# Attention into soft experts on one core: q transposed by PE, scores in 64x32 tiles, phi's sums by two-column products

## The chip, the cores and the metric

The kernel runs on one core of a Trainium2 chip. A time is the device time of one execution in microseconds (us). PE is the matrix engine, DVE, ACT and POOL are the vector, scalar and general engines; SP issues the loads and stores. All data are 32-bit floats.

## The reference

Inputs are q, k, v of shape (8 batches, 8 heads, 576 positions, 64) and phi (8, 8, 576, 32). Phi's softmax pools keys and values to 32 memory slots per head; q attends to those; the result, taken as 4608 rows of 512, goes through a soft mixture of 8 experts with 4 slots each.

```python
a = np.exp(phi - np.max(phi, axis=2, keepdims=True))      # max over the positions
a = a / (np.sum(a, axis=2, keepdims=True) + 1e-09)
k_m = np.einsum('bhsm,bhsd->bhmd', a, k)
v_m = np.einsum('bhsm,bhsd->bhmd', a, v)
scores = scale * np.matmul(q, k_m.transpose(0, 1, 3, 2))
attn = np.exp(scores - np.max(scores, axis=-1, keepdims=True))
attn = attn / (np.sum(attn, axis=-1, keepdims=True) + 1e-09)
x = np.matmul(attn, v_m)                                  # then (b*s, h*d)
logits = x @ phi_moe
d = softmax(logits, over rows); slot_input = d.T @ x
slot_out[e] = np.maximum(slot_input[e] @ w1[e], 0.0) @ w2[e]
return softmax(logits, over slots) @ slot_out
```

## The kernel before, in words

The 8 batches go in four pairs. A batch's q, k, v and phi lie with 128 partitions = two heads x 64 row groups, four quarters c of two heads each, and 9 consecutive positions j per row group (P = 128, HALF = 64, Y = M = 32, J = 9, C = 4).

For each batch, `pool_phi` takes the maximum of phi over positions (DVE L511, PE transposes and broadcasts it at L519 and L533, ACT copies it at L544), subtracts it on POOL (L549) and exponentiates on ACT (L555). The sum over positions is a tree of four additions on POOL (L562) and one product with a mask on PE (L572); DVE forms the reciprocal (L579, L580). `pool_kv` multiplies phi's exponentials with k and v on PE, 72 products in 64x32 tiles, into the two banks of `kvbank` (L599); ACT scales the sums out by the reciprocal (keys L615, values L622). PE transposes the keys (L635, four blocks) and values (L640), ACT copies them (L654, L645), and `vpp` prepares values against the expert router's weights (L662, copied at L675).

q is transposed by DVE in 32x32 blocks (L700), two instructions per batch. That puts the two halves of the 64 head dimensions beside each other, so a score is the sum of two products with 32-deep key blocks; the keys are padded with zeros to hold one 32-row block apart from the other (`kps`, cleared once at L419), and each set of scores (one quarter c of a pair) is 8 products in 64x64 tiles into `scbank` (L716). DVE transposes the set (L730), and `softmax` runs over DVE (L746, L761, L770, L777), POOL (L751, L774) and ACT (L756, L766). `logits` multiplies by the prepared values (L785). After each pair, `route` forms the pair's share of the expert input (L803 to L922, among it the products at L849, L875 and L909). When the last pair is in, SIM, the experts' input, is finished on DVE (L1000); the experts follow on PE (L1064, L1113) with weights of 1 MB each, and the output is formed (L1220) and stored.

What sets the order: every step is handed to a `Plan` with an engine, an assumed cost and its inputs and outputs. The planner plays the program through with those costs, takes for each engine the ready step of the lowest phase, and writes the instructions out in that order; the order on every engine is fixed before the run. Buffers come from pools (`Slots`); a step waits for a free one. `b_m` has three PSUM banks, `b_l` one for the logits, `b_s2` one pair of banks (`scbank`) for the scores, `b_kv` is `kvbank`. On idle PE the plan puts fill products of ones (L476) in the first 25 us and near the end of the attention. SP issues the loads in plan order; k, v, phi and q have two buffers each, the weights lie over buffers that earlier stages have left.

## Time and profile before

| what | us |
|---|---|
| median of three runs (lowest, highest) | 224.25 (222.32, 224.52) |
| the profiled execution's own time | 221.83 |
| its span, first to last instruction | 220.1 |
| busy: PE / DVE / POOL / ACT | 172.5 / 135.5 / 86.7 / 71.4 |
| granted PE clock, mean | 0.916 |
| read from HBM, written | 66.65 MB, 9.44 MB |

In a row of the timeline stand the start, the length, engine, line, operation, output from input, tile sizes and count, and in brackets how long the engine stood idle before it and what it waited for. A group's row has busy us and mean ns of one instruction. A plain fp32 product is two matmul instructions; a transpose by PE is one. Line numbers of before and of the changed kernel differ by 1 to 25.

### The profile page before, as it was taken

How to read it: one execution, taken by the hardware profiler on the slowest of the kernel's cores; microseconds unless marked ns; L12 is line 12 of the kernel's file. 1: busy time of each engine (PE TensorE's matmuls, PEld its weight loads, DVE VectorE, ACT ScalarE, POOL GpSimd, SP SyncE). 2: the span in 40 equal slices, each digit the busy share in tenths (PEclk: the TensorE clock that was granted, in tenths of full speed). 3: DMA queues.
4: the chain of work that ended last, by engine and by line, in shares of the span. 5: the costliest groups of instructions: out<-in, count | busy, mean ns of one | idle time of the engine just before them, and what ended most of it. 6: DMA issues, size and time to landing. Idle time of an engine off the chain costs nothing.

```text
span 220.1 us, 5624 instructions
## 1 busy us (share of the span) xinstructions
PE 172.5 (78%) x2418; PEld 105.3 (48%) x2418; DVE 135.5 (62%) x230; ACT 71.4 (32%) x182; POOL 86.7 (39%) x85
## 2 busy tenths in 40 slices
PE   8997977695798988598988799629999975599400
PEld 6676745354564654356654387415554340065100
DVE  6825048969459999879658965499102860268500
ACT  2041234542516626337342340201002331168400
POOL 6298019596934992999623641030000000000000
PEclk9999999979699999999969999976999999769755
DMA  6999999999999999999596493999999998049997
GB/s 215 383 395 390 380 392 381 390 380 390 385 388 389 388 406 380 389 392 406 194 410 212 188 420 102 401 350 327 395 413 410 408 409 320 3 179 411 415 415 295
DMA packets 27881, 76.45 MB, mean 347 GB/s; under 512 B 1744, under 2 KB 5840, under 8 KB 27856
## 3 DMA queue, kind: packets, MB, share of 16 engines
q1 hardware_dynamic: 27856, 76.09, 91.1%
q8 instruction: 19, 0.31, 0.6%
q14 instruction: 6, 0.05, 0.1%
HBM read 66.65 MB, written 9.44 MB: 346 GB/s over the span
## 4 chain that ended last, share of the span: by engine, by line
PE 41%; DMA 22%; DVE 14%; POOL 9%; issue 5%; ACT 2%; SPq 1%; DVEq 0%; POOLq 0%
DMA top<-in_q_dram 10%; DMA arena<-in_moe_w_dram 9%; PE bank L1064 7%; PE kvbank L476 6%; PE bank L785 5%; PE scbank L716 4%; PE bank L1220 4%; PE kvbank L599 3%; DMA out_dram<-arena 3%; DVE arena L700 3%; POOL arena L774 3%; POOL arena L562 3%; PE bank L849 2%; PE kvbank L1113 2%; POOL arena L751 2%
## 5 line engine op out<-in xcount | busy, mean ns | idle before, releaser
L549 POOL TENSOR_TENSOR arena<-arena 128x1152 f32<-128x1152 f32 x8 | 21.0, 2632 | 16.0 <-ACT arena L544 13.3
L476 PE MATMUL kvbank<-ones 128*128 128x256 f32 x92 | 25.4, 419 | 2.2 <-ACT arena L622 1.1
L700 DVE STREAM_TRANSPOSE arena<-top 128x1152 f32<-128x1152 f32 x16 | 21.7, 1361 | 7.1 <-DMA top<-in_q_dram 7.1
L774 POOL TENSOR_TENSOR arena<-arena,ssm 128x576 f32<-128x576 f32 x16 | 18.5, 1162 | 15.6 <-DVE ssm L770 15.5
L562 POOL TENSOR_TENSOR arena<-arena 128x128 f32<-128x128 f32 (+2 forms) x32 | 23.4, 731 | 2.3 <-ACT arena L555 0.3
L716 PE MATMUL scbank<-arena 64*64 64x288 f32 x256 | 21.6, 433 | 3.0 <-DVE arena L730 2.5
L785 PE MATMUL bank<-arena 128*128 128x288 f32 x64 | 21.4, 464 | 2.6 <-DVE arena L777 2.6
L751 POOL TENSOR_TENSOR arena<-arena,smx 128x576 f32<-128x576 f32 x16 | 18.4, 1158 | 11.5 <-DVE smx L746 11.5
L599 PE MATMUL kvbank<-arena 64*32 64x128 f32 x1152 | 20.2, 273 | 2.2 <-issue 1.5
L476 PEld LDWEIGHTS kvbank<-ones 128*128 128x128 f32 x92 | 18.1, 207 | 6.7 <-issue 1.6
L511 DVE TENSOR_REDUCE arena<-arena 128x128 f32<-128x1152 f32 x8 | 17.0, 2138 | 5.6 <-DMA arena<-in_phi_dram 5.6
L599 PEld LDWEIGHTS kvbank<-arena 64*32 64x32 f32 x1152 | 16.2, 106 | 6.3 <-issue 3.9
L1064 PE MATMUL bank<-arena,SIM 128*32 128x256 f32 x256 | 16.4, 421 | 3.4 <-DVE SIM L1000 3.4
L1113 PE MATMUL kvbank<-arena 128*32 128x512 f32 x128 | 15.6, 598 | 2.9 <-DMA arena<-in_moe_w_dram 2.9
L730 DVE STREAM_TRANSPOSE arena<-scbank 128x576 f32<-128x576 f32 x16 | 12.2, 765 | 8.9 <-PE scbank L716 8.9
L785 PEld LDWEIGHTS bank<-arena 128*128 128x128 f32 x64 | 12.1, 206 | 8.1 <-DVE arena L777 3.8
L1220 PE MATMUL bank<-sr,cT 128*128 128x512 f32 x36 | 13.2, 505 | 3.1 <-DVE sr L1207 1.4
L1231 DVE COPY arena<-bank 128x512 f32<-128x512 f32 x18 | 11.8, 691 | 4.7 <-DMA out_dram<-arena 2.4
L777 DVE STREAM_TRANSPOSE arena<-arena 128x576 f32<-128x576 f32 x16 | 12.1, 758 | 3.8 <-POOL arena L774 3.7
L716 PEld LDWEIGHTS scbank<-arena 64*64 64x64 f32 x256 | 9.0, 137 | 10.8 <-DVE arena L730 4.5
L756 ACT ACTIVATE arena<-arena 128x576 f32<-128x576 f32 x16 | 11.0, 688 | 8.4 <-POOL arena L751 8.4
L1064 PEld LDWEIGHTS bank<-arena,SIM 128*32 128x32 f32 x256 | 8.6, 121 | 10.7 <-DVE SIM L1000 3.6
(104 smaller groups left out, 234.4 us busy)
## 6 DMA issues: line engine op xcount, KB each, us to landing
arena<-in_moe_w_dram SPq DMA_DIRECT2D x32, 1024.0 KB, 9.9
top<-in_q_dram SPq DMA_DIRECT2D x8, 1152.0 KB, 13.8
arena<-in_k_dram SPq DMA_DIRECT2D x8, 1152.0 KB, 11.2
arena<-in_v_dram SPq DMA_DIRECT2D x8, 1152.0 KB, 13.6
out_dram<-arena SPq DMA_DIRECT2D x12, 768.0 KB, 7.6
arena<-in_phi_dram SPq DMA_DIRECT2D x8, 576.0 KB, 8.7
arena<-in_moe_phi_dram SPq DMA_DIRECT2D x1, 64.0 KB, 4.8
```

What stands on the lines that cost most here:

```text
L476: lambda: nc.tensor.matmul(warm.ap, ones, ones.unsqueeze(1).to_broadcast([P, 2, P]), start=True, stop=True,),
L549: lambda: nc.gpsimd.tensor_tensor(ph(), ph(), mb.ap.unsqueeze(2).to_broadcast([P, C, J, M]), op=ALU.subtract),
L562: plus = lambda o, x, y: nc.gpsimd.tensor_tensor(o, x, y, op=ALU.add)
L599: nc.tensor.matmul(acc.ap[M * c: M * c + M, a, : 2 * D], ph()[h0: h0 + HALF, c, j, :], kv()[h0: h0 + HALF, :, c, j * D: j * D + D], start= ...
L700: nc.vector.transpose(qT.ap.rearrange("p (i u y) -> p u i y", i=2, y=Y), qt.ap[:, h * QT_SZ: h * QT_SZ + QT_SZ].rearrange("p (u i x) -> p ...
L716: nc.tensor.matmul(scb.ap[HALF * g: HALF * g + HALF, a, :JY], kb[g].ap[h0: h0 + HALF, i, c].rearrange("p r m -> p (r m)"), qT[g][c // 2].a ...
L751: lambda: nc.gpsimd.tensor_tensor(exv(), exv(), bc(mx), op=ALU.subtract),
L774: lambda: nc.gpsimd.tensor_tensor(exv(), exv(), bc(sm), op=ALU.mult),
L785: nc.tensor.matmul(lp.ap[:, :JY], vpb.ap[:, h, :], aT.ap[:, a * JY: (a + 1) * JY], start=(h == 0), stop=(h == H - 1),)
L1064: nc.tensor.matmul(hb.ap[NS * j: NS * j + NS, :256], SIM.ap[:, 2 * i + c, NS * e: NS * e + NS], wv[:, c, 256 * j: 256 * j + 256], start=(e ...
L1113: nc.tensor.matmul(pacc.ap[NS * x: NS * x + NS, 0, :DM], hT()[:, 4 * t + 2 * i + j, NS * e: NS * e + NS], wv[:, j, t, :], start=(e == 0 an ...
L1220: lambda po=po, i=i, ct=cT[bp, j0]: nc.tensor.matmul(po.ap[:, :DM], ct.ap()[:, i * P: i * P + P], sr.ap, start=True, stop=True),
```

## The change

Four things change together.

q: each batch's q is transposed by PE in 128x128 blocks, two positions of one head pair at a time (L707); the ninth position of two quarters is done by two plain products with the identity (L699). Three blocks go into one of two new PSUM slots, `b_q`, the last 384 columns of each bank of `kvbank`, and ACT copies them out (L712). There are six such groups per batch.

Scores: with all 64 dimensions in partitions a score is one product with the plain keys, in 64x32 tiles: 16 products of 160 or 128 columns per set (L733). Even and odd positions lie apart, DVE turns the set in two pieces (L746), and `POS` undoes the order of positions at the end. The zero padding of the keys goes; PE transposes two key blocks instead of four (L624).

Phi's sums: POOL's tree goes; PE multiplies each of the 9 positions and 4 quarters of phi's exponentials with the two-column mask, 36 products in 128x32 tiles (L564).

Fill products go to the free columns of `scbank`, 192 columns instead of 256.

```diff
-    b_kv = Slots([kvbank])
+    b_kv = Slots([kvbank], [(10, 1)])
+    b_q = Slots([kvbank[:, i, P:] for i in range(2)], [(10, 1), (10, 1)])
+    b_acc = Slots([kvbank], [(10, 1)], (b_kv, b_q))
...
-    NWARM = 40
+    NWARM = 52
...
-            plus(t, ph()[:, :, 0:4, :], ph()[:, :, 4:8, :])
-            plus(t[:, :, 0:2], t[:, :, 0:2], t[:, :, 2:4])
-            plus(t[:, :, 0], t[:, :, 0], t[:, :, 1])
-            plus(es.ap, t[:, :, 0], ph()[:, :, 8, :])
...
+            for j in range(J):
+                for c in range(C):
+                    nc.tensor.matmul(
+                        sp.ap[M * c: M * c + M, :2], ph()[:, c, j, :], maskhp,
+                        start=(j == 0), stop=(j == J - 1), tile_position=(0, M * c),
+                    )
...
-                nc.vector.transpose(
-                    qT.ap.rearrange("p (i u y) -> p u i y", i=2, y=Y),
-                    qt.ap[:, h * QT_SZ: h * QT_SZ + QT_SZ].rearrange("p (u i x) -> p u i x", i=2, x=Y),
-                )
...
+                    for i in range(3):
+                        o = tp.ap[:, i * P: i * P + P]
+                        k = 3 * x + i
+                        if k == JH:
+                            for c in range(2):
+                                nc.tensor.matmul(
+                                    o[HALF * c: HALF * c + HALF],
+                                    qv[:, 2 * h + c, (J - 1) * D: J * D],
+                                    ident, start=True, stop=True,
+                                    tile_position=(0, HALF * c),
+                                )
+                        else:
+                            c, j = (0, k) if k < JH else (1, k - JH - 1)
+                            nc.tensor.transpose(
+                                o, qv[:, 2 * h + c, 2 * j * D: 2 * (j + 1) * D], ident
+                            )
...
+                    nc.scalar.copy(qT.ap[:, 3 * P * x: 3 * P * (x + 1)], tp.ap)
...
+                    for r in range(R):
+                        for s in range(2):
+                            n, b, _ = blocks(s)
+                            h0, x = HALF * s, HALF * g + Y * r
+                            nc.tensor.matmul(
+                                scb.ap[x: x + Y, s, n * Y * a: n * Y * a + n * Y],
+                                kb[g].ap[h0: h0 + HALF, a, c, :],
...
+            turn(0)
+            turn(1)
...
-                add(DVE, dve(QT_SZ), f, r=[qt], w=[t])
+                        add(PE, 0.36, f, r=[qt.part(h), ident_b], w=[tp], also=[t])
+                        add(ACT, act(3 * P), copy, r=[tp], w=[part])
```

What the planner makes of it is seen at two places on PE and one on ACT. On PE right after the scores of pair 0's last quarter, before:

```order
L716 MATMUL scbank<-arena 64x288 x8
L662 MATMUL bank_62<-mphd,arena 64x64 x4
L785 MATMUL bank_65<-arena 128x288 x4
L599 MATMUL kvbank<-arena 32x128 x72
L519 MATMUL bank_63<-ident,arena 128x128
L572 MATMUL bank_64<-maskhp,arena 128x2
L533 MATMUL bank_62<-ident,pmh_82 64x128 x2
L785 MATMUL bank_65<-arena 128x288 x2
```

Changed, from the same place:

```order
L707 MATMUL kvbank<-ident,top 128x128 x4
L699 MATMUL kvbank<-ident,top 64x128 x2
L707 MATMUL kvbank<-ident,top 128x128
L624 MATMUL bank_63<-ident,arena 128x128 x2
L631 MATMUL bank_62<-ident,arena 128x128
L520 MATMUL bank_64<-ident,arena 128x128
L707 MATMUL kvbank<-ident,top 128x128 x6
L807 MATMUL bank_65<-arena 128x288 x2
```

Pair 1's q blocks now stand between the keys' transposes, phi's maximum and pair 0's logits, where before the next pooling followed.

On PE ahead of pair 3's first scores (`top` is q, `kvbank` the pooled sums and the q blocks), before:

```order
L785 MATMUL bank_65<-arena 128x288 x2
L599 MATMUL kvbank<-arena 32x128 x24
L875 MATMUL bank_62<-rep,arena 128x32 x4
L881 MATMUL bank_62<-rep,arena 128x32 x2
L572 MATMUL bank_64<-maskhp,arena 128x2
L909 MATMUL bank_63<-arena 64x128 x4
L785 MATMUL bank_65<-arena 128x288 x2
L635 MATMUL bank_62<-ident,arena 128x4x32 x4
L640 MATMUL bank_64<-ident,arena 128x128
L716 MATMUL scbank<-arena 64x288 x8
```

Changed:

```order
L564 MATMUL bank_64<-maskhp,arena 32x2 x36
L592 MATMUL kvbank<-arena 32x128 x72
L807 MATMUL bank_65<-arena 128x288 x2
L707 MATMUL kvbank<-ident,top 128x128
L699 MATMUL kvbank<-ident,top 64x128 x2
L707 MATMUL kvbank<-ident,top 128x128 x4
L624 MATMUL bank_63<-ident,arena 128x128 x2
L631 MATMUL bank_62<-ident,arena 128x128
L807 MATMUL bank_65<-arena 128x288 x2
L707 MATMUL kvbank<-ident,top 128x128 x3
L653 MATMUL bank_64<-mphd,arena 64x64 x4
L733 MATMUL scbank<-arena 32x160
```

Phi's sums stand ahead of the pooling instead of behind it, and q groups between the last pooling and the scores.

On ACT ahead of the same scores (`prs` is phi's reciprocal), before:

```order
L615 ACTIVATE arena<-kvbank,prs_85 128x4x32 x2
L622 ACTIVATE arena<-kvbank,prs_85 128x64 x2
L922 COPY arena<-bank_63 128x128
L766 ACTIVATE ssm_81<-ssm_81 128x18
L654 COPY arena<-bank_62 128x512
L645 COPY arena<-bank_64 128x256
L675 COPY arena<-bank_63 32x8x32 x2
```

Changed:

```order
L712 COPY arena<-kvbank 128x384 x2
L788 ACTIVATE ssm_81<-ssm_81 128x18
L608 ACTIVATE arena<-kvbank,prs_85 128x128 x2
L613 ACTIVATE arena<-kvbank,prs_85 128x64 x2
L712 COPY arena<-kvbank 128x384 x2
L636 COPY arena<-bank_62 128x256
L645 COPY arena<-bank_63 128x256
L712 COPY arena<-kvbank 128x384
L666 COPY arena<-bank_64 32x8x32 x2
```

The q copies (L712) stand in front of, between and behind the steps that take the pooled sums out, and behind exponentials of the scores (L778).

On SP the loads keep their order but for one weight load, which moves from behind batch 5's q to ahead of batch 5's phi, k and v, and one that now stands between the q loads of batches 6 and 7.

More of the change, by code (lines that the diff above doesn't have):

```diff
@@ L324 @@
     PHI_SZ, KV_SZ = C * J * M, 2 * C * J * D
-    Q_SZ, QT_SZ = C * J * D, C * J * D // 2
-    KP_W = R * (P + Y)
+    Q_SZ, QT_SZ = C * J * D, J * P
+    JH = J // 2
+    QB = J * P
+    POS = [j // 2 if j % 2 == 0 else (J + 1) // 2 + j // 2 for j in range(J)]
     EX_SZ = PC + JN
@@ L466, in first @@
         return FIRST.index(name) - 90000 if name in FIRST else None
-    warm = Tile(ap=kvbank[:, 1, 256:512])
+    warm = Tile(ap=scbank[:, 1, 320:512])
     def fill(n, pri, r=()):
@@ L652, in pool_kv @@
         add(
-            ACT, act(4 * P),
-            lambda: nc.scalar.copy(kd.ap.rearrange("p i c r m -> p (i c r m)"), tp.ap),
+            ACT, act(2 * P),
+            lambda: nc.scalar.copy(kd.ap.rearrange("p a c m -> p (a c m)"), tp.ap[:, : 2 * P]),
             r=[tp], w=[kd],
@@ L685, in load_q @@
     def load_q(b):
-        qt = qs.tile()
+        qt = qs.tile().split(2)
         load(
@@ L696, in q_blocks, with f, copy @@
         for h in range(2):
-            qT = qTs.tile()
-            def f(h=h, qT=qT):
-                nc.vector.transpose(
-                    qT.ap.rearrange("p (i u y) -> p u i y", i=2, y=Y),
-                    qt.ap[:, h * QT_SZ: h * QT_SZ + QT_SZ].rearrange("p (u i x) -> p u i x", i=2, x=Y),
-                )
-            halves.append((qT, f))
+            qT = qTs.tile().split(3)
+            for x in range(3):
+                tp = b_q.tile()
+                def f(h=h, x=x, tp=tp):
+                    qv = qt.ap.rearrange("p (c j d) -> p c (j d)", c=C, j=J)
+                    for i in range(3):
[11 more added lines that the diff above has]
+                            c, j = (0, k) if k < JH else (1, k - JH - 1)
+                            nc.tensor.transpose(
+                                o, qv[:, 2 * h + c, 2 * j * D: 2 * (j + 1) * D], ident
+                            )
+                def copy(x=x, tp=tp, qT=qT):
+                    nc.scalar.copy(qT.ap[:, 3 * P * x: 3 * P * (x + 1)], tp.ap)
+                halves.append((h, qT, qT.part(x), tp, f, copy))
         return halves
@@ L727, in scores, with blocks @@
-        add(PE, 1.0, f, r=[qT[0][c // 2], qT[1][c // 2], *kb], w=[scb], also=[ex])
-        add(
-            DVE, dve(PART),
-            lambda: nc.vector.transpose(
-                ex.ap[:, c * PART: (c + 1) * PART].rearrange("p (a x) -> p a x", a=2),
-                scb.ap[:, :, :JY],
-            ),
-            r=[scb], w=[ex.part(c)],
-        )
+        def blocks(s):
+            n = JH + (s == c % 2)
+            b = 0 if c % 2 == 0 else JH + 1 - s
+            pos = 0 if s == 0 else J - n
+            return n, b, pos
@@ new lines, in f @@
+        def f():
+            for a in range(2):
+                for g in range(2):
+                    for r in range(R):
[5 more added lines that the diff above has]
+                                kb[g].ap[h0: h0 + HALF, a, c, :],
+                                qT[g][c // 2].ap.rearrange("p (b x) -> p b x", b=J)[
+                                    h0: h0 + HALF, b: b + n,
+                                    HALF * a + Y * r: HALF * a + Y * r + Y,
+                                ],
+                                start=True, stop=True, tile_position=(h0, x),
+                            )
@@ new lines, in scores, with turn, f @@
+        add(PE, 0.6, f, r=[qT[0][c // 2], qT[1][c // 2], *kb], w=[scb], also=[ex])
+        def turn(s):
+            n, _, pos = blocks(s)
+            nc.vector.transpose(
+                ex.ap[:, c * PART: (c + 1) * PART].rearrange("p (a x) -> p a x", a=2)[
+                    :, :, pos * Y: (pos + n) * Y
+                ],
+                scb.ap[:, s, : 2 * n * Y].rearrange("p (a x) -> p a x", a=2),
+            )
+        def f():
+            turn(0)
+            turn(1)
+        add(DVE, 2 * dve(PART // 2), f, r=[scb], w=[ex.part(c)])
@@ L939 @@
             qt = load_q(2 * bp + g)
-            hs.append([(qt, *x) for x in q_blocks(qt)])
+            hs.append((qt, q_blocks(qt)))
         for h in range(2):
@@ L943 @@
             for g in range(2):
-                qt, t, f = hs[g][h]
-                add(DVE, dve(QT_SZ), f, r=[qt], w=[t])
-        qT = [[x[1] for x in y] for y in hs]
+                qt, blocks = hs[g]
+                for half, t, part, tp, f, copy in blocks:
+                    if half == h:
+                        add(PE, 0.36, f, r=[qt.part(h), ident_b], w=[tp], also=[t])
+                        add(ACT, act(3 * P), copy, r=[tp], w=[part])
+        qT = [[y[0][1], y[3][1]] for _, y in hs]
         ex = sexs.tile().split(C)
@@ L1051, in load_w @@
         return t
-    pacc = b_kv.tile()
+    pacc = b_acc.tile()
     def expert_in(e, hb):
```

56 lines of the change are left out of this document (13 added, 43 removed).

## The prediction

> **What bounds the kernel now.** I read the chain of waits from its end first, since it says which stretch fixes the time.
>
> ```profile
> 20.63 0.63 ACT arena L615 x2
> 21.26 0.42 ACT arena L622 x2
> ...
> 147.32 0.30 DVE SIM L1000
> 147.67 10.18 PE bank L1064 x144
> ...
> 158.21 6.18 PE bank L1064 x112
> ...
> 168.59 18.81 DMA arena<-in_moe_w_dram
> ...
> 200.37 7.29 DMA out_dram<-arena
> ```
>
> From SIM on, at 147.6 us, the end is a row of expert products, expert weights still arriving, and output. The change touches none of that, so I let those 72.5 us (220.1 less 147.6) stand and ask when SIM is ready. The next view is the busy time by stretches; two are cut at the first scores (L716) of pair 0 and of pair 3. Its columns after the stretch are its length, then busy us of PE, weight loads, DVE, ACT and POOL, granted clock, DMA share, GB/s.
>
> ```profile
> 50.00:60.00 10.00, 5.90 (x140) 4.29 (x130) 7.44 (x12) 3.30 (x10) 8.11 (x8) 0.83 1.06 389
> ...
> 80.00:90.00 10.00, 7.72 (x106) 4.35 (x104) 8.56 (x15) 4.37 (x13) 5.59 (x4) 1.00 1.03 385
> 31.30:114.60 83.30, 68.43 (x1333) 44.23 (x1331) 67.20 (x103) 36.60 (x101) 60.16 (x54) 0.94 1.01 378
> 114.60:135.60 21.00, 19.23 (x169) 12.55 (x169) 15.00 (x26) 6.52 (x20) 9.16 (x8) 1.00 0.67 257
> ```
>
> In the 83.3 us from 31.3, the first scores of pair 0, to 114.6, those of pair 3, three pairs of batches go round. No engine is full: PE 68.4, DVE 67.2, POOL 60.2. PE's 68.4 at a mean clock of 0.94 are 64.3 us of full-clock work; the other 19.0 are 14.9 of standing still and 4.1 of cold clock. What it stands still for, and one wait of ACT's and one of the loads', are in the list of waits (total us, times, longest):
>
> ```profile
> ACT arena L615 <- PE kvbank L476: 4.2, 1, 4.2
> ...
> PE bank L519 <- DVE arena L511: 5.9, 5, 2.4
> ...
> PE bank L785 <- DVE arena L777: 2.6, 4, 1.8
> ...
> PE scbank L716 <- DVE arena L730: 2.5, 5, 0.9
> SPq L458 <- PE kvbank L599: 46.0, 7, 10.4
> ```
>
> PE waits for DVE above all, so taking work off DVE and POOL can help; but the k and v loads wait for PE's pooling (L599), so PE's own queue paces the supply. The bound is the weave of three engines, and the change moves work to one that has 15 us left.
>
> **The change part by part.** The prices of PE come from starts in its timeline, one row's start to the next row's:
>
> ```profile
> 15.78 2.24 PE L599 MATMUL kvbank<-arena 64*32 64x128 f32 x144
> 17.95 1.13 PE L476 MATMUL kvbank<-ones 128*128 128x256 f32 x4
> ...
> 28.69 0.84 PE L599 MATMUL kvbank<-arena 64*32 64x128 f32 x34 [0.66 <-issue]
> ...
> 31.31 1.46 PE L716 MATMUL scbank<-arena 64*64 64x288 f32 x16
> ...
> 60.80 0.68 PE L662 MATMUL bank<-mphd,arena 128*64 128x64 f32 x8
> 61.41 1.24 PE L785 MATMUL bank<-arena 128*128 128x288 f32 x4
> ...
> 64.41 1.20 PE L716 MATMUL scbank<-arena 64*64 64x288 f32 x16
> 65.54 0.28 PE L810 MATMUL bank<-ident,arena 128*32 128x128 f32 x1
> ...
> 68.06 0.66 PE L635 MATMUL bank<-ident,arena 128*128 128x128 f32 x4
> 68.56 0.27 PE L640 MATMUL bank<-ident,arena 128*128 128x128 f32 x1
> ...
> 78.58 0.66 PE L909 MATMUL bank<-arena 128*64 128x128 f32 x8
> 79.17 1.24 PE L785 MATMUL bank<-arena 128*128 128x288 f32 x4
> 80.25 0.28 PE L572 MATMUL bank<-maskhp,arena 128*128 128x2 f32 x2
> 80.45 0.85 PE L599 MATMUL kvbank<-arena 64*32 64x128 f32 x38
> ...
> 100.30 0.60 PE L635 MATMUL bank<-ident,arena 128*128 128x128 f32 x4
> 100.73 0.27 PE L640 MATMUL bank<-ident,arena 128*128 128x128 f32 x1
> ...
> 114.61 1.73 PE L716 MATMUL scbank<-arena 64*64 64x288 f32 x16
> ...
> 139.17 1.65 PE L849 MATMUL bank<-arena 64*32 64x288 f32 x36 [1.16 <-DVE m L969]
> ```
>
> *q by PE.* Half a batch is 8 transposes of 128x128 and two plain 64-column products (four instructions, since a plain fp32 product is two). L635 makes four such transposes in 0.50 us (68.06 to 68.56), 0.43 at best (100.30 to 100.73); L909 eight such instructions in 0.59. So 8 x 0.125 + 4 x 0.074 = 1.3 us, and a pair has four halves: +5.2 us.
>
> *Scores.* A set takes 1.13 us now (64.41 to 65.54). The new one is 32 instructions of 144 columns on average, on eight tiles. L599 does 144 on eight such tiles with 128 columns in 2.17 us, 15.1 ns each, so 17 ns here: 0.54 us. L849, the same tiles with 288 columns read in runs of 32 as the new ones are, takes 1.65 for 36; halved for the columns 23 ns: 0.73. I take 0.62, between. Four sets: -2.0 us.
>
> *Keys.* Two transposes less per batch: 4 x 0.125 = -0.5 us per pair.
>
> *Phi's sums.* One product of 0.20 us (80.25 to 80.45) goes; 36 products, 72 instructions of two columns on four tiles, come. Bounds: L599's 15.1 ns gives 1.09 us per batch, and L1064, four tiles with 256 columns, 6.18/112 = 55 ns, gives 3.97. I take 18 ns, 1.3 us, near the lower end: the weight loads are as wide as L599's, and the 128 columns that fill its time shrink to two. Two batches: +2.2 us. [...]
>
> Together 5.2 - 2.0 - 0.5 + 2.2 = +4.9 us of PE per pair, 14.7 for three: 64.3 + 14.7 = 79.0 of the old 83.3. (Lowest +3.6: transposes 0.43 for four, scores 0.54, sums 1.09. Highest +10.6: scores 0.73, sums 3.97.)
>
> ```profile
> L562 POOL TENSOR_TENSOR arena<-arena 128x128 f32<-128x128 f32 (+2 forms) x32 | 23.4, 731 | 2.3 <-ACT arena L555 0.3
> L700 DVE STREAM_TRANSPOSE arena<-top 128x1152 f32<-128x1152 f32 x16 | 21.7, 1361 | 7.1 <-DMA top<-in_q_dram 7.1
> ...
> L730 DVE STREAM_TRANSPOSE arena<-scbank 128x576 f32<-128x576 f32 x16 | 12.2, 765 | 8.9 <-PE scbank L716 8.9
> ...
> L1175 ACT CAST cT<-bank 128x384 fp32r<-128x384 f32 x12 | 5.1, 484 | 8.1 <-PE bank L1170 8.1
> ...
> L955 DVE STREAM_TRANSPOSE L<-bank 128x288 f32<-128x288 f32 x4 | 1.9, 480 | 4.9 <-PE bank L785 4.9
> ```
>
> *The other engines.* DVE loses L700, 21.7/4 = 5.4 us per pair, and turns the scores in two pieces of about 0.48 (L955) instead of one of 0.765: +0.2 a set, 0.8 a pair. 67.2 - 3 x 4.6 = 53. POOL loses L562, 5.9 a pair: about 43. ACT gains 12 copies of 128x384 a pair, 0.484 each (L1175): +5.8, about 54. So in this stretch all three have at least 29 us to spare and PE becomes the longest queue. What ends PE's waits is then ACT and the banks: the new q blocks lie in the two banks of kvbank behind the pooled sums. That work on other columns there holds a reader up is in the list above (L615 waited 4.2 us for fills, L476, that wrote other columns); so a q block behind a pooling waits for the pooled sums to be scaled out, 0.63 + 0.42 = 1.05 us (L615, L622), and a pooling for the last q copies. I count one such wait uncovered per pair, 1.0, plus 0.4 for turning scores (two pieces, no second score bank) and 0.4 for a q copy queued on ACT behind an exponential that POOL has not fed: 1.8, 5.4 for three. Cold clock in the old ratio, 4.1/14.9 of that: 1.5. The stretch becomes 79.0 + 5.4 + 1.5 = 85.9 us, 2.6 longer.
>
> *Start and end.* Ahead of 31.3 nothing changes: the last piece of pair 0's pooling (28.69) waited for nothing that PE does, it is v still arriving; the new q blocks and sums fit where fills run now. Cover gone, batch 1's sums alone would cost 1.3. One weight load now stands ahead of batch 5's phi, k and v: 1 MB at 385 GB/s (the row 80 to 90), 2.7 us. I put it at nothing, since two buffers let a load run ahead of its pooling; without that cover it costs its 2.7 us. From 114.6 to SIM: four sets save 2.0, their turning costs 0.8, pair 3's second q halves take about 0.4 of the path: -0.8. Key padding and its DVE memsets go at nothing, in the wait for the first phi.
>
> ```profile
> span 220.1 us, 5624 instructions
> ```
>
> So SIM is 2.6 - 0.8 = 1.8 us later: span 221.9. The profiled execution took 221.83 for its 220.1, and the median of the runs, 224.25, stands 2.4 above it: 223.6 by the profile, 226.0 by the median.
>
> **The rivals.** About 1%, 2.2 us, is what a measurement here can tell from no change.
>
> *Forecast: PE takes the bound over and gives back what DVE and POOL save.* 226, its own range 222 to 230. Chance 0.48, of it 0.25 within 1%, 0.19 above, 0.04 below.
>
> *PE runs almost without a stop.* For it: PE's waits above are nearly all for DVE, which gets 14 us back, and q blocks can go wherever PE would stand. Against: every queue is in a fixed order, and the banks are shared. With the low costs, 64.3 + 10.8 = 75.1, 2 us of standing, 0.5 cold: 77.6, 5.7 shorter, and -0.8 at the end: 217.8. Chance 0.28.
>
> *The two-column products do not overlap (slower).* Their place is L564, ahead of each pooling, so they stand before the k and v loads as well. L662's instructions, all on one tile, take 76 ns (60.80 to 61.41, eight); if only two of the four tiles run at once, 38 ns, 2.74 us per batch, 1.44 more for each of six batches: 8.6, 234.6. It decides from about 20 ns on. Against: L1064's 55 ns for 256 columns needs all four at once. Chance 0.15.
>
> *The clock falls.* PE at 59% busy was granted 0.83 (50 to 60), at 77% 1.00 (80 to 90). [...] Half of 79.0 us at 0.83 costs 79.0 x 0.5 x 0.205 = 8.1, less the 1.5 counted: 232.6. Chance 0.09. [...]
>
> **The numbers.** Predicted 226. Faster: 0.04 + 0.28 = 0.32; within 1%: 0.25 and 0.01 of the last two, 0.26; slower: 0.42. The range 217 to 235 leaves out the ends of the first and third rivals' costs.
>
> **What would show it.** In the new profile L564 should take about 1.3 us per batch, L733 0.62 a set, three L707 0.38; first scores of pair 3 near 117 us, SIM near 149; PE 90% or more busy between, DVE, ACT and POOL under 65%; 72 to 73 us from SIM to the end. First scores of pair 3 before 112 make the second case true; L564 over 1.6 us the third; a clock under 0.9 with PE busy the fourth. The forecast is wrong in kind if SIM moves and the end doesn't, or if PE waits more than 10 us for ACT.

## The result, and the profile after

The changed kernel takes 266.82 us, the kernel before 224.03 beside it: a ratio of 1.189, with a 95% interval of 1.177 to 1.200. I had predicted 226.0, with a range of 217 to 235. The profiled execution took 266.59 us for a span of 264.8. Here and below a time is the median of all runs, while a ratio leaves out the runs that fell in a second, slower state.

The same cuts as before, at the first scores of pair 0 and of pair 3 and at SIM, in the view by stretches of the changed kernel (length, busy us of PE, weight loads, DVE, ACT, POOL, granted clock, DMA share, GB/s):

```profile
0.00:41.50 41.50, 32.15 (x560) 25.11 (x561) 9.51 (x17) 13.30 (x31) 9.53 (x14) 0.84 0.85 303
41.50:156.10 114.60, 90.42 (x2077) 64.45 (x2075) 56.68 (x106) 49.01 (x134) 43.18 (x30) 0.84 0.74 266
156.10:192.60 36.50, 25.39 (x299) 16.07 (x296) 21.54 (x44) 9.15 (x30) 11.19 (x9) 0.86 0.68 253
192.60:264.80 72.20, 50.11 (x462) 23.14 (x462) 29.70 (x63) 18.44 (x37) 0.00 (x0) 0.88 0.84 336
```

The first row grew from 31.3 to 41.5 us, the stretch of three pairs from 83.3 to 114.6, the third from 33.0 to 36.5; the fourth is 72.2 where it was 72.5. All 45 us were lost ahead of SIM. In the stretch PE is busy 90 of 114.6 us, at a clock of 0.84 where it was 0.94. The list of waits of the changed kernel for PE in that stretch (total, times, longest) names what it stands still for:

```profile
PE kvbank L592 <- issue: 16.2, 8, 3.2
PE kvbank L707 <- ACT arena L712: 2.4, 3, 0.9
PE kvbank L707 <- ACT arena L613: 1.9, 2, 1.2
PE scbank L733 <- DVE arena L746: 1.9, 3, 1.0
```

L592 is the pooling (L599 before). "Issue" means that nothing shown was awaited. The page of the changed kernel has the whole run, group by group, and the traffic of the queues:

```profile
q8 instruction: 26, 0.43, 0.7%
...
L592 PE MATMUL kvbank<-arena 64*32 64x128 f32 x1152 | 26.2, 322 | 21.6 <-issue 19.9
```

The line for q8 counts packets that carry instructions, 26 of them; the kernel before has this line:

```profile
q8 instruction: 19, 0.31, 0.6%
```

PE's timeline of the changed kernel at the first stop and at two later ones shows where it stands (start, us, what; in brackets the idle time ahead):

```profile
15.27 0.55 PE L707 MATMUL kvbank<-ident,top 128*128 128x128 f32 x3 [0.62 <-ACT arena L712]
15.65 1.47 PE L477 MATMUL scbank<-ones 128*128 128x192 f32 x8
17.05 0.78 PE L564 MATMUL bank<-maskhp,arena 128*32 128x2 f32 x72
17.75 1.34 PE L592 MATMUL kvbank<-arena 64*32 64x128 f32 x76
22.74 2.35 PE L592 MATMUL kvbank<-arena 64*32 64x128 f32 x68 [3.64 <-issue]
...
45.03 0.77 PE L733 MATMUL scbank<-arena 64*32 64x160 f32 x32 [1.00 <-DVE arena L746]
45.80 0.78 PE L564 MATMUL bank<-maskhp,arena 128*32 128x2 f32 x72
49.69 3.38 PE L592 MATMUL kvbank<-arena 64*32 64x128 f32 x128 [3.11 <-issue]
54.52 0.45 PE L592 MATMUL kvbank<-arena 64*32 64x128 f32 x16 [1.45 <-issue]
```

The stops are in the middle of one row of products, once after 76, once before the first, once after 128. The trace shows nothing that is awaited there. Counting all PE records of the trace (each fp32 product is two MATMUL and two LDWEIGHTS: the eight poolings of 72 products are 1152 of each), and setting beside them the packets of the instruction queue, 16,384 bytes each, gives:

```
PE's record   multiple of 256   PE stands (us)        packet in flight   PE after landing
at the stop   behind 449
   449            0             19.09 to 22.74  3.64   20.22 to 21.33      1.40 us
   705            1             26.03 to 26.59  0.56   24.11 to 25.20      1.38
  1473            4             46.58 to 49.69  3.11   47.22 to 48.31      1.38
  1729            5             53.07 to 54.51  1.45   52.11 to 53.19      1.32
  2241            7             71.84 to 74.56  2.72   72.18 to 73.29      1.27
  2753            9             88.05 to 88.71  0.66   86.19 to 87.29      1.42
  3009           10             90.74 to 92.44  1.70   89.75 to 90.97      1.47
  3777           13            108.28 to 110.26 1.98  107.73 to 108.80     1.46
  4289           15            126.34 to 129.52 3.18  127.01 to 128.12     1.40
  5057           18            148.65 to 150.06 1.40  147.60 to 148.69     1.37
```

Every stop lies at a multiple of 256 records, and every time PE goes on 1.3 to 1.5 us after a packet has landed. Together 20.4 us, of which 19.8, all but the stop at 26.03, lie on the chain of work that ended last. I read them as PE having run out of instructions.

The kernel before stops so twice, 0.66 us at record 705 and 0.83 at 2497, again 256 times 1 and 8 behind 449. The first is the row at 28.69 that the prediction quotes; its packet was in flight from 26.09 to 27.18, and PE went on 1.5 us later. The second is this row:

```profile
82.14 0.43 PE L599 MATMUL kvbank<-arena 64*32 64x128 f32 x10 [0.83 <-issue]
```

The rest of this document calls that *standing*: idle time of PE at such a multiple (within 3 records, since a few are missing) that ends 1.1 to 1.7 us after an instruction packet lands.

### The profile page after: what moved, and what is told of

Read it like the earlier page. It is cut to its first block, busy times and chain, and to the rows that moved or that the text cites. A ratio compares the mean times of both kernels' runs of the same rounds, so it can differ in the third digit from the quotient of the medians.

```text
span 264.8 us, 7589 instructions
## 1 busy us (share of the span) xinstructions
PE 198.1 (75%) x3388; PEld 128.8 (49%) x3388; DVE 117.4 (44%) x228; ACT 89.9 (34%) x230; POOL 63.9 (24%) x53
## 4 chain that ended last, share of the span: by engine, by line
PE 59%; DMA 11%; issue 9%; DVE 8%; ACT 6%; POOL 1%; DVEq 0%; ACTq 0%
PE kvbank L592 10%; PE kvbank L707 9%; DMA arena<-in_moe_w_dram 7%; PE bank L807 6%; PE bank L1089 6%; PE scbank L733 4%; PE scbank L477 4%; PE bank L871 3%; ACT arena L712 3%; PE bank L1245 3%; DMA out_dram<-arena 3%; PE kvbank L699 3%; PE bank L653 2%; PE kvbank L1138 2%; PE bank L564 2%
## 5 line engine op out<-in xcount | busy, mean ns | idle before, releaser
L592 PE MATMUL kvbank<-arena 64*32 64x128 f32 x1152 | 26.2, 322 | 21.6 <-issue 19.9
L707 PE MATMUL kvbank<-ident,top 128*128 128x128 f32 x128 | 28.8, 337 | 6.8 <-ACT arena L712 4.7
L592 PEld LDWEIGHTS kvbank<-arena 64*32 64x32 f32 x1152 | 21.0, 124 | 25.0 <-issue 22.2
L712 ACT COPY arena<-kvbank 128x384 f32<-128x384 f32 x48 | 21.6, 483 | 28.5 <-PE kvbank L707 27.4
L707 PEld LDWEIGHTS kvbank<-ident,top 128*128 128x128 f32 x128 | 17.2, 164 | 18.2 <-ACT arena L712 8.8
L796 POOL TENSOR_TENSOR arena<-arena,ssm 128x576 f32<-128x576 f32 x16 | 18.4, 1158 | 27.9 <-DVE ssm L792 27.9
L746 DVE STREAM_TRANSPOSE arena<-scbank 128x320 f32<-128x320 f32 (+1 forms) x32 | 13.5, 460 | 18.6 <-PE scbank L733 14.5
L477 PE MATMUL scbank<-ones 128*128 128x192 f32 x70 | 18.0, 402 | 1.9 <-DVE ones L420 1.1
L608 ACT ACTIVATE arena<-kvbank,prs 128x128 f32<-128x128 f32 x16 | 5.0, 364 | 37.0 <-PE kvbank L592 25.6
L807 PEld LDWEIGHTS bank<-arena 128*128 128x128 f32 x64 | 12.7, 218 | 7.1 <-DVE arena L799 3.4
L477 PEld LDWEIGHTS scbank<-ones 128*128 128x128 f32 x70 | 14.3, 236 | 3.5 <-DVE ones L420 1.1
L733 PE MATMUL scbank<-arena 64*32 64x128 f32 (+1 forms) x512 | 13.1, 301 | 1.9 <-DVE arena L746 1.9
```

The source lines that it names most:

```text
L477: lambda: nc.tensor.matmul(warm.ap, ones, ones[:, :96].unsqueeze(1).to_broadcast([P, 2, 96]), start=True, stop=True,),
L592: nc.tensor.matmul(acc.ap[M * c: M * c + M, a, : 2 * D], ph()[h0: h0 + HALF, c, j, :], kv()[h0: h0 + HALF, :, c, j * D: j * D + D], start= ...
L707: nc.tensor.transpose(o, qv[:, 2 * h + c, 2 * j * D: 2 * (j + 1) * D], ident)
L712: nc.scalar.copy(qT.ap[:, 3 * P * x: 3 * P * (x + 1)], tp.ap)
L733: nc.tensor.matmul(scb.ap[x: x + Y, s, n * Y * a: n * Y * a + n * Y], kb[g].ap[h0: h0 + HALF, a, c, :], qT[g][c // 2].ap.rearrange("p (b x ...
L796: lambda: nc.gpsimd.tensor_tensor(exv(), exv(), bc(sm), op=ALU.mult),
```

## The experiments

Two theories stood first. A: the 144 records a batch of phi's sums, run through in 0.70 us, and the pooling's 288 right behind them use up the packets faster than they come. B: q's blocks lie in the pooling's banks, and the loads of k, v and q, which wait for PE, come late for that. Line numbers differ a little from kernel to kernel: the pooling is L590, L592, L593, L596, L601 or L602 in the rows below.

One thing limits what the runs can tell. When the planner is given other steps or costs, it writes another order for every engine; so it is in tree, before72, sums18, before18, tcopy2, tnoqplan, tnoq0 and tplan. In wide, quarter, shift, tnoq, tnocopy and split the order is the one of the kernel that was edited, but for what is added or left out.

| run | what it is | us | ratio to before, 95% |
|---|---|---|---|
| tree | changed, phi's sums by POOL again | 249.62 | 1.116 [1.108, 1.125] |
| before72 | before, with phi's 72-record sums alone | 246.29 | 1.098 [1.091, 1.106] |
| sums18 | changed, sums by 128-column products | 254.42 | 1.135 [1.129, 1.141] |
| before18 | before, sums by 128-column products | 229.92 | 1.028 [1.019, 1.037] |
| shift | changed, 124 records more ahead | 265.27 | 1.175 [1.168, 1.183] |
| wide | changed, sums 128 columns wide | 260.28 | 1.153 [1.145, 1.162] |
| quarter | changed, a quarter of the loads | 251.98 | 1.113 [1.102, 1.124] |
| tcopy2 | tree, half the q copies on DVE | 249.72 | 1.106 [1.097, 1.115] |
| tnoq | tree, no q blocks from pair 1 on | 236.75 | 1.060 [1.049, 1.072] |
| tnocopy | tree, no q copies from pair 1 on | 240.36 | 1.071 [1.062, 1.080] |
| tnoqplan | tnoq, order written anew | 233.60 | 1.044 [1.032, 1.055] |
| tnoq0 | tnoqplan, pair 0's q by DVE | 237.48 | 1.058 [1.048, 1.067] |
| tplan | tree, order written anew | 256.55 | 1.142 [1.131, 1.152] |
| split | before, scores' products cut in two | 227.34 | 1.014 [1.003, 1.024] |
| qdve | before, new scores and keys alone | 228.18 | 1.021 [1.015, 1.028] |

### One part at a time

*tree* undoes the sums:

```diff
-        for j in range(J):
-            for c in range(C):
-                nc.tensor.matmul(sp.ap[M * c: M * c + M, :2], ph()[:, c, j, :], maskhp, ...)
+        plus(t, ph()[:, :, 0:4, :], ph()[:, :, 4:8, :])
...
+        nc.tensor.matmul(sp.ap[:, :2], es.ap.rearrange("p c m -> p (c m)"), maskhp, ...)
```

> The changed kernel with one part undone: phi's sums go back to the tree of four additions on POOL and one product on PE, so that 144 PE instructions (72 products and their weight loads) leave each batch; q's transposes, the copies and the new scores stay. Theory A (instruction supply: PE's instructions come in packets of 256, and PE stands wherever it runs through a packet in less than about 5 us): PE has 5666 instructions in place of 6818, the idle 'issue' time ahead of the pooling products falls from 19.9 us to under 4, and the time falls to 226 to 242 us. Rival B (q's copies and the pooling share the two banks of kvbank, and the loads of k, v and q come late for that): the sums are only 0.7 us a batch of PE, and the time stays at 255 us or more.

*before72* is the same edit the other way round, in the kernel before.

> The kernel before with this part of the change alone: phi's sums by 72 two-column products a batch on PE, POOL's tree gone; q is still transposed by DVE and the scores are the old ones. Theory A: PE has 1152 instructions more, now stands still inside the pooling at every second or third packet, and the time rises to 236 to 252 us, with 8 to 20 us of 'issue' ahead of the pooling products. Rival B: nothing of q's has been touched, so kvbank is free as before; the sums cost 0.7 us a batch at most and the time is 222 to 231 us.

tree took 249.62, between the two expectations; before72 took 246.29, where only A had it. The list of waits of before72 has one great row for PE, and its timeline shows the same picture with q untouched:

```profile
PE kvbank L590 <- issue: 25.3, 7, 5.0
```

```profile
42.46 0.78 PE L562 MATMUL bank<-maskhp,arena 128*32 128x2 f32 x72
43.17 1.37 PE L590 MATMUL kvbank<-arena 64*32 64x128 f32 x80
49.57 1.75 PE L590 MATMUL kvbank<-arena 64*32 64x128 f32 x56 [5.03 <-issue]
```

So the sums alone, 0.71 us of PE a batch, cost 21.5 us: 25.6 of standing against 1.5 before, more than the 8 to 20 that A expected. A is right for them. But tree is 24.8 us over the kernel before with the sums gone, and PE stands for only 7.3 of its span by the count above. More than half of the loss has a second cause, taken up further below.

### More work in fewer or longer instructions

*sums18* has the sums made by 9 products whose weights are the two columns of the mask and whose 128 columns are phi's; the result is turned back by one transposition.

```diff
-            for c in range(C):
-                nc.tensor.matmul(sp.ap[M * c: M * c + M, :2], ph()[:, c, j, :], maskhp, ...)
+            nc.tensor.matmul(sp.ap[:2, :P]..., maskhp, ph()[:, :, j, :], start=(j == 0), stop=(j == J - 1))
...
+        nc.tensor.transpose(st2.ap[:, :2], sg.ap[:2, :P], ident[:2, :2])
```

> The changed kernel, all of it, with the sums of phi's exponentials by 9 products of 128 columns (two columns of weights) and one transposition back, 20 PE instructions a batch in place of 144; PE is busy with them for 0.9 to 1.5 us a batch by the 128-column rows (longer than the 0.7 us of the 72 small products), and DVE gets a copy more. Theory A: although PE has more to do, the standing goes and the time falls to 228 to 245 us. Rival B: nothing that q does is changed, PE's work is some 4 us longer: 265 to 275 us.

The expectation's 20 instructions count a product once; the trace has 106 records a batch less, 38 in place of 144. The products were dearer than I had written, 20.0 us in all against 6.9 for the small ones:

```profile
L566 PE MATMUL bank<-arena,maskhp 128*2 128x128 f32 x144 | 20.0, 302 | 1.3 <-ACT arena L557 1.3
```

With 13 us more to do PE finished 12.4 us earlier: standing fell from 20.4 to 9.5. The time is over A's range. tree, without the dearer products, is over it as well (249.62), so the second cause is enough for that.

*before18* makes the same edit in the kernel before.

> The kernel before with POOL's tree replaced by the 9 products of 128 columns and the transposition back: 18 PE instructions a batch more than before. Theory A: no new standing of PE (its two stalls of 0.7 and 0.8 us may move); PE's 0.9 to 1.5 us a batch against POOL's relief: 220 to 232 us. Rival B says the same. The run tells what taking the tree from POOL is worth when it is done without many instructions: under 223 us if the tree held the pooling up, over 228 if PE is all that counts.

It took 229.92, over 228: 5.1 us slower for 18.4 us of products on PE. "No new standing" was wrong: its trace has 5.0 us, 2.95 at record 449 and 2.06 at 1217, against 1.5 before. So the run doesn't tell what taking the tree from POOL is worth by itself.

*wide* keeps the number of instructions and makes each longer:

```diff
-    sp.ap[M * c: M * c + M, :2], ph()[:, c, j, :], maskhp,
+    sp.ap[M * c: M * c + M, :P]..., ph()[:, c, j, :], maskhp.unsqueeze(1).to_broadcast([P, P // 2, 2]),
```

> The changed kernel with the columns of phi's sums repeated 64 times: 128 columns in place of two per product, the same number of instructions, the same sums in the columns that are used. By the pooling's rows (64x128 in 15 ns on eight tiles, so about 30 ns on four) PE has 1.3 to 1.6 us more work a batch, 10 to 13 us in all. Theory A: where PE stands for a packet the longer work fills the standing, and the time rises by 0 to 5 us over the changed kernel's 266.8. Rival (PE's work counts in full): 277 to 280 us.

The groups of the changed kernel and then of wide (busy us, mean ns, idle ahead):

```profile
L564 PE MATMUL bank<-maskhp,arena 128*32 128x2 f32 x576 | 6.9, 176 | 1.1 <-issue 0.6 <-ACT arena L556 0.5
```

```profile
L564 PE MATMUL bank<-maskhp,arena 128*32 128x128 f32 x576 | 18.1, 278 | 0.5 <-ACT arena L556 0.5
...
L593 PE MATMUL kvbank<-arena 64*32 64x128 f32 x1152 | 21.6, 281 | 16.8 <-issue 15.7 <-ACT arena L713 1.2
```

PE was given 11.2 us more work in L564, and the kernel became 6.5 us faster, outside both ranges. Standing fell by 4.7. The pooling itself fell from 26.2 to 21.6 us though its products are the same, and the mean clock rose from 0.851 to 0.895. I had not foreseen that a longer instruction can come with a faster clock; that the shorter standing is what raised it is not shown (more on this further below).

### Where the stops are, and what makes a packet late

*shift* puts instructions without use ahead of everything:

```diff
+    def pad():
+        for i in range(32):
+            x = M * (i % C)
+            nc.tensor.matmul(scbank[x: x + M, 0, :2], ones[:, :M], ones[:, :2], ...)
```

> The changed kernel with 32 two-column products of constants ahead of everything (results unused, under 1 us at the start while PE only warms up) and two filling products fewer by the plan: 124 PE instructions more in front of all the work. Theory A (packets of 256): the stalls stay at PE's instruction 449 and multiples of 256 behind it, so the first one moves against the work by 124 instructions: PE stands after some 14 of the records of the first pooling group in place of 76. All later stalls stand elsewhere in the work too, the time changes by a few us either way, 255 to 275. Rival B (a dependency or an event of the pooling itself): the first stall stays behind 76 records of the pooling group.

All eight stops moved in the work and none in the count: records 705, 1217, 1729, 2497, 3009, 3777, 4545, 5313 are 256 times 1, 3, 5, 8, 10, 13, 16, 19 behind 449. The expected place of the first was wrong, since the packet at 449 now came in time, and PE stopped at the next multiple, with 142 of the pooling's 144 records done:

```profile
17.82 2.23 PE L602 MATMUL kvbank<-arena 64*32 64x128 f32 x142
23.87 0.41 PE L602 MATMUL kvbank<-arena 64*32 64x128 f32 x2 [3.82 <-issue]
```

A dependency of the pooling would not move so. PE stands for 23.5 us in all, and the time is that of the changed kernel: moving the stops about doesn't help by itself.

*quarter* asks why a packet is late at times and not at others. In the traces of before, after, tree, before72 and sums18, a packet's transfer begins 1.06 us (median of 18, at most 1.7) after the first record of the packet ahead of it where the DMA engines were under 10% busy in the 1.5 us before, and 2.87 us (median of 80, at most 7.1) where they were over 90% busy; it then takes about 1.1 us. If the data transfers cause that, fewer of them must shorten the standing.

```diff
-    load(lambda i=i: kv()[:, i], rows(src, b), ...)
+    n = C if b < 2 else 1
+    load(lambda i=i, n=n: kv()[:, i, :n], rows(src, b)[:, :n], ...)
```

> The changed kernel with a quarter of the bytes of the loads of k, v and q from the third batch on (three of four heads' pairs of rows left out; the data of earlier batches are used again): the DMA engines are mostly idle in the loop. Theory A with the rule read from the traces so far (a packet's fetch starts 1.1 us after the packet ahead of it is entered where no data moves, and 2.9 us, up to 7, where the engines are full): PE's standing falls from 21.7 us to 5 to 12 us, the time to 245 to 258 us. Rival D (the loop waits for its loads): the standing stays and the time falls by more than the standing does, to under 245 us. Rival E (fetches are no faster): standing and time stay within 4 us.

251.98 us, within A's range, and the list of waits of quarter has:

```profile
PE kvbank L596 <- issue: 10.7, 8, 3.6
```

Standing fell from 20.4 to 11.3 us, as A had it (in a profiled execution of 255.75 us, 3.8 over the median of quarter), 3.6 of it at the first stop, where nothing was changed. With the engines quiet the quickest packets of the changed kernel follow each other at 3.5 to 3.7 us (they start at 52.11 and 55.63, at 89.75 and 93.47), about the sum of 1.06 to the start, 1.1 of transfer and 1.4 until PE goes on. That fewer loads shorten the standing, in the same order of work, is shown. What holds a packet up while data move is not seen in the records.

### The other half: q by PE and the new scores

tree is 24.8 us over the kernel before. *tcopy2* was to tell whether the two-slot handoff between PE and ACT costs it:

```diff
+    e = DVE if (h + x) % 2 else ACT
...
+    if e == DVE:
+        nc.vector.tensor_copy(o, tp.ap)
```

> The run tree (the changed kernel with POOL's tree of sums, 249.6 us) with every second of the 48 copies of q's groups on DVE in place of ACT. In tree PE waits 7.9 us in the loop for these copies, since there are two slots for them. Theory Q1 (the two-slot handoff from PE to ACT and back is what makes q dear): that wait halves and the time falls by 3 to 8 us, to 241 to 247 us. Rival Q2 (PE's own time for the blocks, 23.3 us in the loop where 15.6 were reckoned, and the loads that come later for it): within 2 us of tree, or slower since DVE's own chain is in the way.

No change: 249.72, in an order written anew. So spreading the copies over two engines brought nothing here; it doesn't follow that they cost nothing. *tnoq* and *tnocopy* leave work out where `skip` is set, from the second pair on; tnocopy has the second of these lines alone:

```diff
-    add(PE, 0.36, f, ...)
-    add(ACT, act(3 * P), copy, ...)
+    add(PE, 0.36, (lambda f=f, skip=skip: None if skip else f()), ...)
+    add(ACT, act(3 * P), (lambda f=copy, skip=skip: None if skip else f()), ...)
```

> The run tree (249.6 us) without q's blocks on PE and their copies on ACT from the second pair of batches on (36 of 48 groups left out; the scores there use the first pair's q). Theory Q2 (PE's own time for the blocks with its share of waits is what makes the q part 25 us dearer than the kernel before; the loads come later only because PE frees their buffers later): in tree's loop the blocks are 23.3 us of PE and 7.8 us of waits for copies, so the time falls by 20 to 30 us, to 220 to 230. Rival Q3 (the price is in the new scores, their two transpositions on DVE, or the loads): it falls by less than 12 us, to 238 or more.

> The run tree without ACT's copies of q's groups from the second pair on (the blocks stay on PE, which overwrites its slots without waiting for ACT). Theory Q2: only the waits of PE for the copies go, 7.8 us in the loop: 240 to 247 us. Theory Q1 in a wider form (ACT's 0.48 us copies, 36 of them, hold up ACT's other work and the pooling with it): 225 to 238 us. No price in the copies at all: within 2 us of tree.

tnocopy came within Q2's range: 9.3 us less. Its list of waits has 1.4 us of PE's q blocks waiting for these copies where tree's has 8.3. tnoq fell by 12.9, less than Q2 said and just past Q3's line: 12 us stay, in a kernel whose PE has no more to do than the one before. *tnoqplan* and *tnoq0* look for these in the order and in the start:

```diff
-    if half == h:
+    if half == h and bp == 0:
```

> The run tnoq (236.75 us: tree without q's blocks and copies from the second pair of batches on), but the planner too doesn't know of the blocks that are left out, so that the order of all queues is written for a kernel without them. If the order that the planner wrote around q's blocks holds up the rest (theory O): PE has the new scores and 8 us less to do in the loop than the kernel before, and the time falls to 220 to 229 us. If what is left of the q part's price, 12 us, lies in the first pair's blocks and in the packets (theory S): within 3 us of 236.75.

> As tnoqplan, and the first pair's q is turned by DVE as in the kernel before (32x32 blocks, so what the scores read is arranged otherwise): no q block is left on PE, nothing of q on ACT. Theory S: the first scores come at 31 to 33 us again (37.8 in tnoq, 31.3 before), and the time is 5 to 8 us under tnoqplan's. If the start's delay is given back later: within 2 us of tnoqplan.

tnoqplan fell by 3.2 us against tnoq, short of O's range. tnoq0 rose by 3.9 against tnoqplan, which neither expectation had: its first scores come at 33.2 us where tnoqplan's come at 35.9, and the three pairs then take 93.3 us where tnoqplan takes 86.1. *tplan* changes only the number that the planner is given for a q group:

```diff
-    add(PE, 0.36, f, ...)
+    add(PE, 0.53, f, ...)
```

> The run tree (249.62 us) with q's groups entered in the plan at the 0.53 us that the trace showed for them, in place of 0.36; the work is the same, and only the order that the planner writes is another. Theory O: with truer costs the time falls by 4 to 12 us, to 238 to 246. Otherwise: within 3 us of tree.

The truer number gave an order that is 6.9 us worse than tree's, outside both expectations, with the same work but for a few fill products; standing is 12.7 us where tree has 7.3. So the order is worth several us, but not by the rule that I expected. The planner knows nothing of packets.

*split* gives the kernel before the new scores' number of instructions and nothing else:

```diff
-    scb.ap[HALF * g: HALF * g + HALF, a, :JY], ... c % 2, :],
+    scb.ap[HALF * g: HALF * g + HALF, a, n * s: n * s + n], ... c % 2, n * s: n * s + n],
```

> The kernel before with each of its scores' products cut into two of 144 columns: the same work in the same order, the same transpositions by DVE, but a set of scores is 64 PE instructions in place of 32, as it is in the changed kernel (512 more in all). PE's time for a set stays near 1.1 to 1.3 us, at most 0.2 longer, 3 us in all. Theory A (what is left of the q part's price, some 10 us with no q block on PE, is again PE standing for its packets, now for the scores' many short instructions): standing rises from 1.5 to 5 to 14 us and the time by 4 to 14 us over the kernel before. Rival W (the longer list of instructions costs nothing by itself; the rest comes from the two transpositions of each set or from the written order): standing stays under 4 us and the time within 3 us of the kernel before.

It costs 2.0 us, as W had it. The standing is not W's: the trace has 7.6 us, 3.2 of it in one stop at record 1217, where A had 5 to 14 and W under 4. That profiled execution took 233.62 us, 6.3 over the median, so the two numbers can't be set against each other. Last, *qdve* has the new scores and keys with q by DVE, and the compute engines' work in the order of the kernel before:

```diff
-    add(PE, 0.6, f, r=[qT[0][c // 2], qT[1][c // 2], *kb], ...)
-    add(DVE, 2 * dve(PART // 2), f, ...)
+    add(PE, 1.0, f, r=[qT[0][c // 2], qT[1][c // 2], *kb], ...)
+    add(DVE, dve(PART), f, ...)
...
+    add(DVE, dve(QT_SZ), turn, r=[qt], w=[t])
```

> The changed kernel's scores (64x32 tiles, two transpositions by DVE a set) and plain keys alone: q is turned by DVE in 32x32 blocks as before (so the scores meet q in another arrangement), phi's sums are POOL's tree, and the planner is given the costs of the kernel before, so that every compute engine has its operations in the order of the kernel before. tnoq0 had the same scores and keys and no q block on PE, in an order that the planner wrote for it, and took 11.8 us more than the kernel before. Theory O (that order is what costs): 218 to 228 us. Theory I (the scores' own instructions, their packets and transpositions cost it): 232 us or more.

228.18, 0.2 over O's range, well under I's, and 4.8 us over the kernel before. tnoq0 has the same scores and less work on DVE, and is 3.6% further off; what it has besides is another order and 11 more fill products. That the order makes those 8 us is argued from the difference of these two and from tplan; no run changes tnoq0's order alone.

Of tree's 24.8 us, then, 9.3 go with the copies and 3.6 more with the blocks (tnocopy and tnoq, in tree's order). What the other 12 are stays open: that it is the written order is argued, from tplan and qdve.

### Adding it up

One row per profiled execution: span, PE's busy time from the page, standing as defined above, and what is left, PE's waits for other engines and transfers. (One execution a row: quarter, split and tcopy2, whose profiled executions were 2.6 to 6.3 us over their medians, are left out.)

```
            span    PE busy   standing   other idle
before      220.1    172.5      1.5        46.1
before18    227.3    183.1      5.0        39.2
qdve        227.3    171.2      5.4        50.7
tnoqplan    229.4    166.1     12.3        51.0
tnoq        234.5    173.4      8.7        52.4
tnoq0       234.9    173.1     14.5        47.3
tnocopy     238.6    186.5     10.0        42.1
before72    245.0    180.5     25.6        38.9
tree        247.4    186.8      7.3        53.3
sums18      252.6    202.0      9.5        41.1
tplan       255.8    192.8     12.7        50.3
wide        257.5    199.6     15.7        42.2
shift       263.5    195.4     23.5        44.6
after       264.8    198.1     20.4        46.3
```

The changed kernel's 44.7 us are 25.6 of busier PE, 18.9 of standing and 0.2 of other waits. tree's 27.3 are 14.3, 5.8 and 7.2. tnoq0's 14.8 are 0.6, 13.0 and 1.2: with q off PE, what remains there is standing too. The last column follows POOL's tree in part: it is 38.9 to 42.2 in before72, before18, sums18 and wide, where the tree is gone, and 46.1 to 53.3 in the kernels that have it, but tnocopy has the tree and 42.1, and the changed kernel has none and 46.3 (44.6 in shift).

## Why the prediction was wrong

**What held.** SIM to the end: 72.2 us against 72.5. The prices of the instructions by themselves: three L707 in 0.38 us at best (15.27 to 15.65), the sums in 0.70 (17.05 to 17.75) where I had 1.3, a set of scores 0.77 (45.03 to 45.80), a little over the 0.73 that was my upper bound. DVE, ACT and POOL are each under half busy in the stretch. PE's waits there for other engines are 24.2 less 16.2, 8.0 us, against the 5.4 that I put.

**The step that failed first** is "it is v still arriving", said of the row at 28.69. That stop ended 1.5 us after an instruction packet. It was one of two such stops in the old profile (82.14 is the other), and was read as a load; seen as a stop for a packet, it would have made the count of PE's instructions, 40% more records in the new kernel (6818 against 4876), a term of the sum. The sum for the stretch, 79.0 + 5.4 + 1.5 = 85.9, has no such term, and 16.2 us of the stretch and 4.2 of the start are it. What the traces show of it is packets of 16,384 bytes, stops at multiples of 256 records, and a packet that starts to move 1.06 us, or 2.87 with the DMA engines full, in the median, after the first record of the packet ahead.

**The cold clock**, which I put at 1.5 us, was mis-sized, by 13.0 us. By the same working that gave 64.3 before, PE's 90.4 us at 0.84 are 75.9 of full-clock work, 3.1 less than the 79.0 of the sum, and 14.5 of cold clock. So the 114.6 us are 75.9 of work, 14.5 of cold clock, 16.2 of standing and 8.0 of waits for other engines, where the sum had 79.0, 1.5, nothing and 5.4. The pooling took 20.0 us in the stretch for the same 864 records that took 15.3:

```profile
L592 PE MATMUL kvbank<-arena 64*32 64x128 f32 x864 | 20.0, 327 | 16.8 <-issue 16.2 <-ACT arena L712 0.5
L707 PE MATMUL kvbank<-ident,top 128*128 128x128 f32 x88 | 19.6, 335 | 4.4 <-ACT arena L712 2.4 <-ACT arena L613 1.9
...
L699 PE MATMUL kvbank<-ident,top 128*64 128x128 f32 x44 | 5.6, 338 | 0.0
```

The q blocks, 25.2 us for 33 groups of three, are 0.76 a group where 1.3/3 = 0.43 was reckoned (0.65, counted from one start to the next as the prediction did). What made the clock fall stays open; the rivals below say how far the runs go.

**"Ahead of 31.3 nothing changes"** was wrong by 10.2 us, and "from 114.6 to SIM: -0.8" by 4.3. At the start 4.2 us are standing. tree, which has q's blocks and not the sums, has its first scores at 36.6 us, and qdve, which has neither, at 31.2. So the blocks cost 5.4 us where the fills were to give way, 1.8 of it standing (3.05 against 1.28).

**The balance** "64.3 + 14.7 = 79.0 of the old 83.3" let the new work fill PE's old waits, and in the stretch it came out in part: the waits for others went from 14.0 us (14.9 less 0.8 of standing) to 8.0. They are 6.4 in before72 and 6.6 in before18, which have no tree on POOL and q and the scores as before, but 15.3 in tree (101.2 less 81.6 busy and 4.3 of standing), 8.6 of it ended by the copies of q. So new work on PE did not fill the old waits by itself, and no run separates what made them give way in one kernel and not in another. Outside the stretch the changed kernel waits 6.2 us longer than the one before, which the sum did not have either.

**The rivals.** PE did not run almost without a stop. The two-column products overlap: 72 records in 0.70 us are 9.8 ns each, where the forecast had 18 and the rival in which they don't overlap 38. The clock did fall, and the sign that I gave for it, a clock under 0.9, was there. No run shows the half of the stretch at 0.83 that the fourth rival's sum takes: the mean over all of it was 0.84. q's transposes don't explain that. These are the rows of the stretch in tree, with all of q's blocks and no sums on PE, and in before72, with the sums and no q block:

```profile
36.60:137.80 101.20, 81.60 (x1660) 56.39 (x1662) 55.93 (x104) 48.73 (x134) 60.29 (x54) 0.92 0.80 293
```

```profile
36.90:136.80 99.90, 73.86 (x1754) 50.22 (x1752) 67.79 (x104) 36.84 (x101) 43.24 (x30) 0.85 0.79 286
```

And in wide, with the blocks and the sums, and in qdve, with neither:

```profile
39.20:149.30 110.10, 89.08 (x2081) 65.19 (x2080) 56.55 (x106) 49.00 (x134) 43.19 (x30) 0.95 0.77 277
```

```profile
31.20:116.00 84.80, 68.05 (x1513) 47.37 (x1511) 67.40 (x115) 35.39 (x100) 59.24 (x54) 0.83 0.99 367
```

0.92 and 0.95 with the transposes (and 0.84 in the changed kernel), 0.85 and 0.83 without. So the transposes by themselves did not lower it here. Nor did standing by itself: wide stands for 13.6 us of its row and has the highest, qdve for 4.1 and has the lowest. What set it no run here shows.

## What to carry to other kernels

Count PE's instructions, not only their time: here an fp32 product was four, and instruction packets (26 for PE's 6818 records, 19 for the 4876 of before) followed each other at 3.5 to 3.7 us at the quickest, where no data moved, and, by the medians above (2.87 + 1.1 + 1.4), at an estimated 5.4 us where the loads filled the DMA engines. Nine of the ten stops of the changed kernel lie in or ahead of the pooling's short products (15.1 ns each in the kernel before), the tenth in phi's sums, and the profile shows them as "issue", most of them in the middle of a row of equal products. There fewer or longer instructions were faster even with more work in them (wide by 6.5 us with 11.2 more, sums18 by 12.4 with 13), and an "issue" of half a microsecond in a profile is worth following to its cause before instructions are added.

## What the hardware showed that was not expected

- PE stopped at multiples of 256 of its records (counted from 449), for up to 5.0 us (before72), and went on 1.3 to 1.5 us after a 16 KB instruction packet had landed, 1.2 to 1.6 over all runs; where data filled the DMA engines the packet started 2.87 us after the first record of the one ahead, in the median, and 1.06 where they were quiet.
- 11.2 us more of PE's work in instructions of the same number made the kernel 6.5 us faster, and the granted clock rose from 0.851 to 0.895; why it did is open.
- 72 products' records of two columns on four tiles took 9.8 ns each; 128 columns on the same tiles 29.6 ns (17.17 to 19.30 in wide for 72).
